# One-core attention and gated-MLP kernel: chunk 1's transposes moved from TensorE to DMA, the gate weights queued later, score runs joined, and a new instruction order

## The chip, the cores and the metric

The kernel runs on one core of a Trainium2 chip. The metric is device time in microseconds (us). The engines are named as the profile names them: PE (TensorE matmuls; PEld its weight loads), DVE (VectorE), ACT (ScalarE), POOL (GpSimd) and SP (SyncE, which here only issues DMAs). POOL issues DMAs too.

## The reference

```python
def layernorm(x): return (x - mean(x)) / sqrt(var(x) + 1e-5)

# x is 1 x 2048 x 512, bf16
q, k, v = split(layernorm(x) @ wqkv)           # 32 heads of 16 channels
# each position s attends to 8 positions: s, s-2, s-4, ..., s-14 (those below 0 masked)
logits = einsum("bhsd,bhswd->bhsw", q, k_gathered) * 16 ** -0.5
o = einsum("bhsw,bhswd->bhsd", softmax(logits), v_gathered)
h = x + o @ wo
gate, up = layernorm(h) @ W_gate, layernorm(h) @ W_up    # 512 -> 1376
out = h + (relu(gate) * up) @ W_down                     # 1376 -> 512
```

## The kernel before

The 2048 positions are worked in four chunks (`tk` 0 to 3) of 512, each of four blocks of 128 rows (`j` 0 to 3). In each chunk:

- `layernorm` makes the normed rows (tiles `row`; steps `xst`, `xag`, `xrl`, `xre`, `xn`). They are then transposed, channels onto partitions, into a `quad` tile `[128, 4, 512]`. Which way a pair of blocks is turned is listed in `DMAT`: a listed pair is turned by DMA transposes that SP issues (`f_td`, L533), any other on PE (`f_tp`, L544), whose PSUM bank is then copied out by ACT or, for block 1 of chunk 0, by DVE (`f_ev`, L558 and L560). Before, `DMAT` has chunk 3's second layernorm input of the attention (`('x',3,0)`, `('x',3,2)`) and all four second layernorms (`'h'`), not chunk 1's.
- The q, k and v projections (L585) run on PE, four matmuls of 512 columns to a bank, and ACT copies each bank out (L593). For chunk 0 the first six q and k banks are filled in parts as the blocks arrive: part `a` is block 0, `d` block 1, both with the first two weight tiles; `b` the other two weight tiles for blocks 0 and 1; `c` and `e` blocks 2 and 3.
- DVE multiplies q with shifted k (L636, L651 in chunk 0), for two halves (`hf` 0 and 1) of four shifts each. PE sums the products over channels with the 0/1 matrix `sel`: four matmuls of 32 output rows side by side in the array (`tile_position`). These are the **score runs** (`f_sc`, L642; L694 where DVE has added two products first, `PRE`). Each half had a run of its own. ACT takes the exponential (L708) into an `ex` tile.
- PE sums the exponentials (L725), ACT inverts the sum (L731, L734), `ex` is spread over partitions by DMAs (L768, from SP and POOL), and DVE multiplies with shifted v (L800, L815). The eight products are summed by DMAs that accumulate, issued by POOL (L843), and by DVE (L803), into the output tile `OT` (L807, L837).
- PE applies `wo` (L881), DVE adds x (L892), the second layernorm follows (ACT L457, DVE L510, DMA transposes), and then the MLP: up and gate matmuls (L954; the last 96 channels L921), ACT copies (L958, L961), DVE product (L982), down matmuls (L1005) and the output.

All weights are loaded by SP's queue. Before, `wo` (L348) and the gate half of `wgu_sb` (L349) go out in `setup`; the names in `LATE` (`u`, `d`) are loaded when chunk 0's attention is through.

What sets the order of the instructions: every step is an `Op` with an engine and a planned duration. `Plan.order` takes the steps by the numbers in `RANK`, gives each a planned start (from planned durations such as `SW`, the cost of a score run beyond its matmuls, and planned arrival times `XT` and `WT` of the blocks of x and the weights), and the program is written out by planned start. Each engine then works through its own list in that order and waits on semaphores; nothing overtakes on an engine or on SP's queue.

Of the kernel before, what the change touches and what calls it, by code (L numbers as in the profile page):

```python
# [8 lines left out]
P = 128  # L9
# [4 lines left out]
ALU = mybir.AluOpType  # L14
# [187 lines left out]
def kernel(  # L202
# [27 lines left out]
    LATE = "ud"  # L230
# [75 lines left out]
    def f_load(n, i):  # L306
        if n == "d":
            lo, hi = (0, 5) if i == 0 else (5, NFF)
            nc.sync.dma_start(
                wd_sb[:, lo:hi, :], B_W_down[lo * P:hi * P, :].rearrange("(ft p) n -> p ft n", p=P))  # L310
            if FTAIL and i:
                nc.sync.dma_start(wd_sb[:FTAIL, NFF, :], B_W_down[NFF * P:F, :])
        else:
            w = B_W_up.rearrange("(dt p) f -> p dt f", p=P)
            nc.sync.dma_start(wgu_sb[:, 2 * i:2 * i + 2, 1, :], w[:, 2 * i:2 * i + 2, :])

    def setup():
# [31 lines left out]
        nc.sync.dma_start(wgu_sb[:, :, 0, :], B_W_gate.rearrange("(dt p) f -> p dt f", p=P))  # L349

# [29 lines left out]
    XT = (3.45, 3.65, 4.05, 5.3, 7.15, 8.65, 9.0, 9.4, 13.0, 14.5)  # L380
    WT = (8.35, 8.35, 7.0, 10.85, 15.8, 25.5, 19.2, 29.0)
    DMAT = (('h',0,0),('h',0,2),('h',2,0),('h',2,2),('h',3,0),('h',3,2),('h',1,0),('h',1,2),('x',3,0),('x',3,2))
# [8 lines left out]

    BCN = 4
# [4 lines left out]
    TMT = (0, 1, 2, 3)  # L397
    TTM, DTG, ATE = 0.0825, 0.27, 0.225
# [6 lines left out]
    SW = 0.21  # L405
# [24 lines left out]
    fills = [add(("warm", 0), "PE", 5.6, f_warm, [], -500, take=[wb])]  # L430

# [8 lines left out]
    def layernorm(tk, src, dst_slots, pr, groups, on_act, residual=None):  # L440
# [7 lines left out]
        for grp in groups:  # L448
# [78 lines left out]
            for j0 in range(lo, hi, step):  # L527
# [24 lines left out]
                tev = not residual and tk == 0 and j0 == 1  # L552
# [15 lines left out]
    for tk in range(NCK):  # L568
# [52 lines left out]
        kp = {t: kdone.get((tk - 1, t)) for t in range(NT)}  # L621
        for hf in range(2):
# [55 lines left out]
            elif (tk, hf) in PRE:  # L678
# [19 lines left out]
                scd = [add(("sc%d" % hf, tk), "PE", nu * MM + SW, f_sc, [a], apr, take=[sc], use=[prd[0][1]], lat=PEL)]  # L698
# [8 lines left out]
            def f_ex(sc=sc, ex=ex):  # L707
                nc.scalar.activation(out=ex.t[:], in_=sc.t[:], func=ACT.Exp, scale=SCALE)  # L708

            def f_mk(hf=hf, ex=ex):  # L710
                V.tensor_tensor(out=ex.t[:, 0:PADL], in0=ex.t[:, 0:PADL], in1=mask[:, hf, :],
                                op=ALU.mult)

            a = add(("ex%d" % hf, tk), "ACT", A5, f_ex, scd, apr, take=[ex], use=[sc], lat=AL)
            if tk == 0:
                a = add(("mk%d" % hf, tk), "DVE", DSM, f_mk, [a], apr, use=[ex], lat=DL)
# [378 lines left out]
```

## Time and profile before

| | before |
|---|---|
| three runs | 191.16, 191.26, 192.79 us; median 191.26 us |
| span of the profiled execution | 190.2 us, granted clock 0.998 |
| between span and median | 1.06 us |
| busy: PE, DVE, ACT, POOL | 185.1, 150.7, 113.5, 25.2 us |
| PE matmuls | 1127 |

A row of the timeline reads: start and duration in us, engine, line, operation, output<-input, shape, count, and in brackets the idle time just before and what ended it. The duration of a group runs to the end of its last instruction; successive matmuls overlap, so what a matmul costs is the distance from one start to the next. The span is that of the one profiled execution; no time outside the profile is given for it, so it stands beside the median of the three runs with 1.06 us around it.

### The profile page before, as it was taken

Reading aid. Unit: us, or ns where it says so; the run is one execution under the profiler, and the core shown is the slowest. Engines: PE = TensorE matmul, PEld = TensorE weight load, DVE = VectorE, ACT = ScalarE, POOL = GpSimd, SP = SyncE. Lnnn points to the kernel's source line nnn. Section 1 sums busy time; section 2 is a strip of 40 time slices with the busy share of each in tenths; the row PEclk is TensorE's granted clock in tenths of the full one; section 3 lists DMA queues with packets and bytes.
Section 4 is the critical chain, followed back from the end, with each engine's and each line's share of the span. In section 5 each row is a group of like instructions: output and inputs, shape, how many; then the busy total and the mean of one; then the engine's idle time right before and its main releaser. Section 6 shows DMA issues by size and latency. Waiting matters only on the chain.

```text
span 190.2 us, 3080 instructions
## 1 busy us (share of the span) xinstructions
PE 185.1 (97%) x1127; PEld 95.4 (50%) x1127; DVE 150.7 (79%) x231; ACT 113.5 (60%) x234; POOL 25.2 (13%) x47
## 2 busy tenths in 40 slices
PE   7799999999999999999999999999999999999993
PEld 7676555554444445544344464444454444455453
DVE  5899999999999999999999998998485712114324
ACT  2579999985467945762483795146466713358500
POOL 4000221400000004230033123027000000000000
PEclk9999999999999999999999999999999999999999
DMA  5999364993198858998438798779922211000503
GB/s 182 281 347 370 90 163 87 191 194 59 21 330 177 233 166 153 194 191 182 83 65 152 142 181 186 180 137 166 221 44 55 55 28 59 28 0 0 165 3 110
DMA packets 27743, 26.98 MB, mean 142 GB/s; under 512 B 14704, under 2 KB 23248, under 8 KB 27728
## 3 DMA queue, kind: packets, MB, share of 16 engines
q1 hardware_dynamic: 23696, 15.34, 29.7%
q0 software_dynamic: 3312, 10.49, 28.6%
q10 hardware_dynamic: 720, 0.95, 1.5%
q8 instruction: 9, 0.15, 0.3%
q14 instruction: 6, 0.05, 0.1%
HBM read 8.42 MB, written 2.10 MB: 55 GB/s over the span
## 4 chain that ended last, share of the span: by engine, by line
PE 82%; ACT 11%; DMA 3%; DVE 1%; issue 1%; SPq 0%
PE bank L954 37%; PE bank L1005 20%; PE bank L585 12%; PE bank L881 7%; ACT row L512 5%; DMA x_sm<-in_A_x_dram 3%; PE bank L921 3%; ACT quad L560 2%; ACT vT L593 2%; PE bank L642 2%; ACT quad L593 1%; PE bank L694 1%; ACT kT L593 1%; ACT ex L708 1%; SPq L323 0%
## 5 line engine op out<-in xcount | busy, mean ns | idle before, releaser
L954 PE MATMUL bank<-quad,wgu_sb 128*128 128x512 bf16 x320 | 72.3, 379 | 0.0
L954 PEld LDWEIGHTS <-wgu_sb 128*128 128x128 bf16 x320 | 30.9, 98 | 37.3 <-issue 1.7
L1005 PE MATMUL bank<-wd_sb,gT 128*128 128x512 bf16 (+3 forms) x198 | 39.7, 355 | 0.0
L958 ACT CAST up_sb<-bank 128x512 bf16<-128x512 f32 x40 | 23.1, 591 | 21.0 <-PE bank L954 14.9
L585 PE MATMUL bank<-quad,wqk_sb 128*128 128x512 bf16 (+2 forms) x176 | 30.4, 321 | 0.5 <-DVE quad L558 0.4
L961 ACT ACTIVATE gr<-bank 128x512 bf16<-128x512 f32 x40 | 23.3, 606 | 9.7 <-PE bank L954 8.2
L1005 PEld LDWEIGHTS <-gT 128*128 128x128 bf16 (+1 forms) x198 | 18.5, 98 | 19.7
L982 DVE TENSOR_TENSOR gT<-gr,up_sb 128x1024 bf16<-128x1024 bf16 x20 | 13.6, 686 | 14.4 <-PE bank L1005 7.0
L636 DVE TENSOR_TENSOR big<-quad,kT 128x4096 bf16<-128x4096 bf16 x11 | 24.8, 2279 | 0.0
L585 PEld LDWEIGHTS <-wqk_sb 128*128 128x128 bf16 x176 | 17.1, 113 | 11.4 <-issue 1.1
L800 DVE TENSOR_TENSOR big<-big,vT 128x4096 bf16<-128x4096 bf16 x9 | 20.4, 2281 | 0.0
L843 POOL DMA_DIRECT2D big<-big x13 | 11.6, 965 | 64.3 <-PE bank L954 32.6
L1013 DVE SCALAR_TENSOR_TENSOR row<-bank,iv,x_sm 128x512 bf16<-128x512 f32 (+2 forms) x10 | 6.3, 643 | 13.4 <-PE bank L1005 13.2
L457 ACT ACTIVATE junk<-x_sm,sm 128x512 bf16<-128x512 bf16 x16 | 11.6, 727 | 8.8 <-DVE x_sm L892 8.8
L585 PE MATMUL bank<-quad,wv_sb 128*128 128x512 bf16 x64 | 16.1, 380 | 0.2 <-ACT quad L560 0.2
L881 PE MATMUL bank<-wo_sb,quad 128*128 128x512 bf16 x64 | 15.0, 379 | 0.0
L892 DVE SCALAR_TENSOR_TENSOR x_sm<-x_sm,bank 128x512 bf16<-128x512 bf16 x16 | 10.8, 678 | 2.4 <-PE bank L881 2.4
L803 DVE TENSOR_TENSOR big<-big 128x1024 bf16<-128x1024 bf16 (+1 forms) x17 | 10.3, 622 | 1.6 <-DMA big<-big 1.4
L467 DVE BATCH_NORM_STATS2 st<-x_sm 128x6 f32<-128x512 bf16 x16 | 10.2, 679 | 1.1 <-DMA x_sm<-in_A_x_dram 1.1
L593 ACT CAST quad<-bank 128x512 bf16<-128x512 f32 x16 | 9.3, 594 | 2.5 <-PE bank L585 2.4
L593 ACT CAST kT<-bank 128x512 bf16<-128x512 f32 x16 | 9.3, 596 | 1.9 <-PE bank L585 1.0
L593 ACT CAST vT<-bank 128x512 bf16<-128x512 f32 x16 | 9.1, 610 | 2.1 <-PE bank L585 2.1
(80 smaller groups left out, 175.6 us busy)
## 6 DMA issues: line engine op xcount, KB each, us to landing
big<-big POOLq DMA_DIRECT2D x13, 512.0 KB, 5.2
big<-ex SPq DMA_DIRECT2D x20, 128.0 KB, 3.1
big<-ex POOLq DMA_DIRECT2D x12, 128.0 KB, 3.8
wgu_sb<-in_B_W_gate_dram SPq DMA_DIRECT2D x1, 1376.0 KB, 9.3
wgu_sb<-in_B_W_up_dram SPq DMA_DIRECT2D x2, 688.0 KB, 5.0
wd_sb<-in_B_W_down_dram SPq DMA_DIRECT2D x2, 640.0 KB, 5.7
x_sm<-in_A_x_dram SPq DMA_DIRECT2D x2, 512.0 KB, 6.2
wqk_sb<-wqk_sb POOLq DMA_DIRECT2D x2, 512.0 KB, 5.8
```

The source lines that it names most:

```text
L457: nc.scalar.activation(out=junk[:, j % 2, :], in_=h.t[:] if h else x_sm[:, tk * BPC + j, :], func=ACT.Square, bias=sm.t[:, j:j + 1], scale ...
L585: nc.tensor.matmul(mm.t[:, lo:hi], lhsT=wv_sb[:, dt, t:D:NT] if c == 2 else wqk_sb[:, dt, c * D + t:(c + 1) * D:NT], rhs=xnT.t[:, dt, lo:h ...
L593: nc.scalar.copy(out=o, in_=mm.t[:])
L636: V.tensor_tensor(out=pb.t[:].rearrange("p (t w) s -> p t w s", t=2), in0=q4, in1=k4, op=ALU.mult)
L800: V.tensor_tensor(out=mt.t[:], in0=ab.t[:], in1=v8, op=ALU.mult)
L843: nc.gpsimd.dma_start(mt.t[:, 0:4, :], mt.t[:, 4:8, :], accum_op=ALU.add)
L881: nc.tensor.matmul(od.t[:], lhsT=OT.t[:, t, j * P:(j + 1) * P], rhs=wo_sb[:, t, :], start=(t == 0), stop=(t == NT - 1 and tk not in RPE))
L954: nc.tensor.matmul(mm.t[:fs, lo:hi], lhsT=wgu_sb[:, dt, g, ft * P: ft * P + fs], rhs=hnT.t[:, dt, lo:hi], start=(dt == 0), stop=(dt == NT ...
L958: nc.scalar.copy(out=ub.t[:fs, i, :], in_=um.t[:fs, :])
L961: nc.scalar.activation(out=gr.t[:fs, i, :], in_=gm.t[:fs, :], func=ACT.Relu)
L982: V.tensor_tensor(out=gt.t[:fs, 0:n, :], in0=gr.t[:fs, 0:n, :], in1=ub.t[:fs, 0:n, :], op=ALU.mult)
L1005: nc.tensor.matmul(od.t[:, c0:c1], lhsT=gts[ft].t[:fs, ft % 2, j * P:(j + 1) * P], rhs=wd_sb[:fs, ft, c0:c1], start=(ft == 0), stop=(ft == ...
```

## The change

Five edits: chunk 1's first layernorm goes into `DMAT` (transposes by SP's DMAs in place of PE and ACT); the gate weights join `LATE` as `g` and their load is planned as a step of SP after `wo`; in the chunks listed in `MS` (1 to 3) both halves' score matmuls become one step, `sc1`; `TEV = ()` lets ACT copy out block 1 of chunk 0 where DVE did; `RANK`, `SW`, `XT` and `WT` have new numbers.

```diff
 RANK = [
-    0, 1, 2, 3, 4, 5, 6, 7, 8, 9, 18, 10, 11, 12, 14, 15, 16, 17, 13, 19,
+    0, 4, 5, 7, 22, 38, 56, 20, 33, 120, 41, 15, 25, 97, 135, 406, 441, 493, 11, 224,
...
-    LATE = "ud"
+    LATE = "udg"
...
+        elif n == "g":
+            nc.sync.dma_start(wgu_sb[:, :, 0, :], B_W_gate.rearrange("(dt p) f -> p dt f", p=P))
...
         nc.sync.dma_start(wo_sb[:], A_wo.rearrange("(p t) f -> p t f", t=NT))
-        nc.sync.dma_start(wgu_sb[:, :, 0, :], B_W_gate.rearrange("(dt p) f -> p dt f", p=P))
-
+        if "g" not in LATE:
+            f_load("g", 0)
...
-    XT = (3.45, 3.65, 4.05, 5.3, 7.15, 8.65, 9.0, 9.4, 13.0, 14.5)
-    WT = (8.35, 8.35, 7.0, 10.85, 15.8, 25.5, 19.2, 29.0)
-    DMAT = (('h',0,0),('h',0,2),('h',2,0),('h',2,2),('h',3,0),('h',3,2),('h',1,0),('h',1,2),('x',3,0),('x',3,2))
+    XT = (3.5, 3.7, 4.6, 6.3, 7.3, 8.3, 8.6, 8.95, 13.1, 14.5)
+    WT = (7.95, 7.95, 6.2, 11.2, 15.8, 25.5, 19.2, 29.0)
+    DMAT = (('h',0,0),('h',0,2),('h',2,0),('h',2,2),('h',3,0),('h',3,2),('h',1,0),('h',1,2),('x',1,0),('x',1,2),('x',3,0),('x',3,2))
...
+    MS = (1, 2, 3)
...
+    TEV = ()
...
-    SW = 0.21
+    SW = 0.19
...
+    if "g" in LATE:
+        wload["g"].append(add(("ldg", 0), "SP", 0.45, lambda: f_load("g", 0), wload["o"], 0, lat=1.0, dq=(1.0, 3.6)))
...
-                tev = not residual and tk == 0 and j0 == 1
+                tev = not residual and tk == 0 and j0 in TEV
...
+        both = []
         for hf in range(2):
...
+            elif tk in MS:
+                both.append((sc, ex, [a for a, _, _ in prd], [b for _, b, _ in prd], 4, lambda p=prd: [f() for _, _, f in p]))
             elif tk in MERGE:
...
+            if tk in MS and hf == 0:
+                continue
+            if tk in MS:
+                a = add(("sc1", tk), "PE", sum(x[4] for x in both) * MM + SW, lambda p=both: [x[5]() for x in p],
+                        [d for x in both for d in x[2]], apr, take=[x[0] for x in both], use=[d for x in both for d in x[3]], lat=PEL)
```

Three places show what the new order does.

**DVE at the start**, chunk 0's first layernorm: `st` and `mv` are statistics of a block of x, `row` its normed rows (`row_104` to `row_107` are blocks 0 to 3; `quad_79<-bank_140` copies block 1's transpose out). Before:

```order
L515 TENSOR_SCALAR row_104<-x_sm,mv_117,rs_129 128x512
L467 BN_STATS st_115<-x_sm 128x6
L515 TENSOR_SCALAR row_105<-x_sm,mv_117,rs_129 128x512
L470 BN_AGGR mv_117<-st_115 128x2
L467 BN_STATS st_116<-x_sm 128x6
L470 BN_AGGR mv_117<-st_116 128x2
L558 COPY quad_79<-bank_140 128x4x128
L515 TENSOR_SCALAR row_106<-x_sm,mv_117,rs_129 128x512
L515 TENSOR_SCALAR row_107<-x_sm,mv_117,rs_129 128x512
```

and of the change:

```order
L478 BN_AGGR mv_117<-st_115 128x2
L478 BN_AGGR mv_117<-st_114 128x2
L523 TENSOR_SCALAR row_104<-x_sm,mv_117,rs_129 128x512
L475 BN_STATS st_116<-x_sm 128x6
L478 BN_AGGR mv_117<-st_116 128x2
L523 TENSOR_SCALAR row_105<-x_sm,mv_117,rs_129 128x512
L523 TENSOR_SCALAR row_106<-x_sm,mv_117,rs_129 128x512
L523 TENSOR_SCALAR row_107<-x_sm,mv_117,rs_129 128x512
```

Block 2's statistics (`st_115`) now precede block 0's rows, block 1's rows stand behind the statistics of block 3 (`st_116`), and the copy is gone from DVE.

**SP's queue** between the loads of `setup` and the second layernorm: `big_92<-ex` are the spreading DMAs of chunk 0, `quad_82<-row` chunk 2's transposes. Before:

```order
L768 DMA big_92<-ex_101 128x1x512 x2
L533 DMA_TRANSPOSE quad_82<-row_107 128x4x128
L533 DMA_TRANSPOSE quad_82<-row_108 128x4x128
L533 DMA_TRANSPOSE quad_82<-row_104 128x4x128
L533 DMA_TRANSPOSE quad_82<-row_105 128x4x128
L315 DMA wgu_sb<-in_B_W_up_dram 128x2x1376 x2
```

and of the change (`quad_81` is chunk 1):

```order
L541 DMA_TRANSPOSE quad_81<-row_106 128x4x128
L541 DMA_TRANSPOSE quad_81<-row_105 128x4x128
L791 DMA big_92<-ex_100 128x1x512 x2
L791 DMA big_92<-ex_101 128x1x512 x2
L541 DMA_TRANSPOSE quad_82<-row_107 128x4x128
L541 DMA_TRANSPOSE quad_82<-row_108 128x4x128
L541 DMA_TRANSPOSE quad_82<-row_105 128x4x128
L541 DMA_TRANSPOSE quad_82<-row_106 128x4x128
L314 DMA wgu_sb<-in_B_W_gate_dram 128x4x1376
L317 DMA wgu_sb<-in_B_W_up_dram 128x2x1376 x2
```

Chunk 1's transposes (the last two are shown) now precede the spreading DMAs, and the gate load has moved behind chunk 2's transposes.

**PE at chunk 1's scores**: `bank_143<-big_92` ends the run of the first half, `wv_sb` is a projection. Before:

```order
L642 MATMUL bank_143<-big_92,sel 32x512
L642 LDWEIGHTS sel
L642 MATMUL bank_143<-big_92,sel 32x512
L585 LDWEIGHTS wv_sb
L585 MATMUL bank_139<-quad_84,wv_sb 128x512
```

and of the change, where `bank_139` is the first half and `bank_142` the second:

```order
L651 LDWEIGHTS sel
L651 MATMUL bank_139<-big_89,sel 32x512
L651 LDWEIGHTS sel
L651 MATMUL bank_142<-big_90,sel 32x512
L651 LDWEIGHTS sel
```

The second half's matmuls now follow the first's at once, where a projection stood between.

More of the change, by code (lines that the diff above doesn't have):

```diff
@@ L696, in f_sc @@
                                              stop=(u == nu - 1), tile_position=(0, g * HB))
-                scd = [add(("sc%d" % hf, tk), "PE", nu * MM + SW, f_sc, [a], apr, take=[sc], use=[prd[0][1]], lat=PEL)]
+                if tk in MS:
+                    both.append((sc, ex, [a], [prd[0][1]], nu, f_sc))
+                else:
+                    scd = [add(("sc%d" % hf, tk), "PE", nu * MM + SW, f_sc, [a], apr, take=[sc], use=[prd[0][1]], lat=PEL)]
+            elif tk in MS:
+                both.append((sc, ex, [a for a, _, _ in prd], [b for _, b, _ in prd], 4, lambda p=prd: [f() for _, _, f in p]))
             elif tk in MERGE:
@@ L705, with f_ex, f_mk @@
                                    take=[sc], use=[pb], lat=PEL))
[L707 to L716, printed above, removed]
-            exs.append(ex)
-            exd.append(a)
+            if tk in MS and hf == 0:
+                continue
+            if tk in MS:
+                a = add(("sc1", tk), "PE", sum(x[4] for x in both) * MM + SW, lambda p=both: [x[5]() for x in p],
+                        [d for x in both for d in x[2]], apr, take=[x[0] for x in both], use=[d for x in both for d in x[3]], lat=PEL)
+                scs = [(h, x[0], x[1], [a]) for h, x in enumerate(both)]
+            else:
+                scs = [(hf, sc, ex, scd)]
+            for h, sc, ex, scd in scs:
+                def f_ex(sc=sc, ex=ex):
+                    nc.scalar.activation(out=ex.t[:], in_=sc.t[:], func=ACT.Exp, scale=SCALE)
+                def f_mk(h=h, ex=ex):
+                    V.tensor_tensor(out=ex.t[:, 0:PADL], in0=ex.t[:, 0:PADL], in1=mask[:, h, :],
+                                    op=ALU.mult)
+                a = add(("ex%d" % h, tk), "ACT", A5, f_ex, scd, apr, take=[ex], use=[sc], lat=AL)
+                if tk == 0:
+                    a = add(("mk%d" % h, tk), "DVE", DSM, f_mk, [a], apr, use=[ex], lat=DL)
+                exs.append(ex)
+                exd.append(a)
         dn, rc = Buf(at_s), Buf(rc_s)
@@ L863 @@
             lg = add(("lg", tk), "DVE", 0.08, f_lg, list(oev.values()), apr, use=[OT], lat=0.1)
-            for n in LATE:
+            for n in LATE.replace("g", ""):
                 for i in range(2):
```

74 rows, old and new, of the table RANK are left out of this document.

## The prediction

> **What bounds the kernel now.** I read the busy table first, then the waits of PE after the start, then the table by stages, and then went to the places that the change touches.
>
> ```profile
> PE 185.1 (97%) x1127; PEld 95.4 (50%) x1127; DVE 150.7 (79%) x231; ACT 113.5 (60%) x234; POOL 25.2 (13%) x47
> PE bank L585 <- ACT quad L560: 0.2, 1, 0.2
> 10.48:37.70 27.22, 27.05 (x200) 16.07 (x200) 27.02 (x45) 25.57 (x47) 5.21 (x8) 1.00 0.74 206
> 37.70:90.00 52.30, 52.30 (x292) 24.94 (x292) 52.05 (x69) 33.58 (x70) 6.34 (x9) 1.00 0.77 173
> 143.00:187.70 44.70, 44.29 (x237) 21.86 (x235) 16.25 (x33) 19.83 (x44) 0.00 (x0) 1.00 0.18 49
> ```
>
> The second row is the whole list of PE's waits from 16 us to the end: one. In the stage rows (length, then busy us of PE, PEld, DVE, ACT, POOL, then granted clock) PE is full in every stage at clock 1.00, so the kernel ends when PE's list is through, and a saving is what leaves that list or closes a gap in it. But DVE is as full until 90 us (27.02 of 27.22, 52.05 of 52.30): PE runs without gaps because its order always has a matmul ready where DVE is late. The two meet at chunk 0's `wo`:
>
> ```profile
> 47.53 0.76 DVE L807 TENSOR_TENSOR quad<-big,rec 128x512 bf16<-128x512 bf16 x2
> 48.29 3.62 PE L881 MATMUL bank<-wo_sb,quad 128*128 128x512 bf16 x16
> ```
>
> DVE writes the last of chunk 0's attention output at 47.53 + 0.76 = 48.29, and `wo` starts at 48.29. A PE that gets there sooner has to wait.
>
> **The change part by part.** The sum is made against the profiled execution's span, 190.2 us; 1.06 us lie between it and the median of 191.26, and I take them as unchanged.
>
> *Transposes leave PE.*
>
> ```profile
> 32.73 0.61 PE L544 MATMUL bank<-identity,row 128*128 128x128 bf16 x8
> 34.95 0.61 PE L544 MATMUL bank<-identity,row 128*128 128x128 bf16 x8
> 35.40 1.92 PE L585 MATMUL bank<-quad,wqk_sb 128*128 128x512 bf16 x8
> ```
>
> Eight cost the distance to the next start, 35.40 - 34.95 = 0.45, or 0.056 each. Chunk 1 has 16 of them: **-0.90**. That is certain, since PE's list is shorter by it.
>
> *Score runs joined.* A run of 16 matmuls in chunk 1, and chunk 2's two runs (timeline rows; the fourth row is a piece of the chain of waits):
>
> ```profile
> 43.74 1.03 PE L585 MATMUL bank<-quad,wqk_sb 128*128 128x512 bf16 x4
> 44.69 1.05 PE L642 MATMUL bank<-big,sel 128*32 128x512 bf16 x16
> 45.67 1.05 PE L585 MATMUL bank<-quad,wv_sb 128*128 128x512 bf16 x4
> 59.27 8.63 PE bank L954 x40
> 67.83 1.05 PE L642 MATMUL bank<-big,sel 128*32 128x512 bf16 x16
> 68.70 0.60 PE L694 MATMUL bank<-big,sel 128*32 128x512 bf16 x8
> ```
>
> A 512-column matmul costs 8.63 / 40 = 0.216. The four at 43.74 are through at 44.60, the run starts at 44.69 (0.09), and its 16, four side by side, are 4 x 0.216 = 0.86 of the 0.98 to the next start (0.12): 0.21 a run beyond its matmuls. But in chunk 2 the second run starts 68.70 - 67.83 = 0.87 after the first: these two are joined already, and nothing goes there. Chunks 1 and 3 save one run each: 2 x 0.21 = **-0.41**, where the edit reads like three.
>
> *ACT's queue in chunk 1.*
>
> ```profile
> 19.83 1.00 ACT L560 COPY quad<-bank 128x1024 bf16<-128x1024 bf16 x1
> 21.20 1.03 ACT L560 COPY quad<-bank 128x1024 bf16<-128x1024 bf16 x1
> 37.16 0.38 PE L725 MATMUL bank<-row,spread 128*128 128x512 bf16 x1
> 37.70 0.59 PE L585 MATMUL bank<-quad,wv_sb 128*128 128x512 bf16 x2 [0.16 <-ACT quad L560]
> ```
>
> Two copies of 1.0 us leave an engine that is 25.57 us busy in 27.22. The one gap that ACT makes on PE, 37.70 - 37.16 - 0.216 = 0.32, should close: **-0.32**, bounds -0.32 and 0.
>
> *The start.* Here the order costs. These rows are before's (timeline; the last but one is from the chain of waits):
>
> ```profile
> 6.23 0.40 DVE L515 TENSOR_SCALAR row<-x_sm,mv,rs 128x512 bf16<-128x512 bf16 x1
> 6.69 0.40 PE L544 MATMUL bank<-identity,row 128*128 128x128 bf16 x4 [0.52 <-DVE row L515]
> 7.33 0.69 DVE L467 BATCH_NORM_STATS2 st<-x_sm 128x6 f32<-128x512 bf16 x1 [0.61 <-DMA x_sm<-in_A_x_dram]
> 7.37 0.83 PE L585 MATMUL bank<-quad,wqk_sb 128*128 128x128 bf16 x12
> 8.15 0.39 DVE L558 COPY quad<-bank 128x512 bf16<-128x512 bf16 x1
> 8.46 0.79 DVE L515 TENSOR_SCALAR row<-x_sm,mv,rs 128x512 bf16<-128x512 bf16 x2
> 9.36 1.07 ACT L560 COPY quad<-bank 128x512 bf16<-128x512 bf16 x2 [0.56 <-PE bank L544]
> 10.48 5.54 PE bank L585 x54
> 15.84 1.89 PE L585 MATMUL bank<-quad,wv_sb 128*128 128x512 bf16 x8
> ```
>
> Block 3 of x lands at 7.3, and its statistics start then in both orders. Before, block 1's rows were made at 6.23, ahead of that wait, and PE filled it at 7.37 with part `a` of six banks. Now block 1's rows stand behind it: they take the copy's place at 8.15 (so moving the copy to ACT by itself costs and saves nothing on DVE), block 2's follow at 8.46 and block 3's at 8.85, as before. Block 1's transpose starts at about 8.59 and not 6.69. ACT then has three copies in a row from 9.03 at 0.49 each (1.07 for two less the overlap), the last to 10.59, and PE, which has the transposes and three parts `a` still to do, reaches the matmuls that need it at about 10.68 rather than 10.48. Behind that point stand 5.36 us in the old order (15.84 - 10.48), and 0.33 more now, the six 0.056 us matmuls of part `a` that no longer fit ahead of it. Chunk 0's q and k end at 10.68 + 5.36 + 0.33 = 16.37 rather than 15.84: **+0.53**. Bounds: 0, if block 3 lands early enough to cover it, and +0.9, if a copy more slips.
>
> *Chunk 1 by DMA.* Four transposes run beside nothing at 120 us and beside the up weights at 52 us:
>
> ```profile
> L533 SPq DMA_TRANSPOSE quad<-row x4: 1212/1220/1222, 120.8 to 124.7; - x4
> DMA to landing us min/median/max: 2.5/2.5/2.5
> DMA to landing us min/median/max: 2.6/3.9/5.2
> 16.52 2.93 ACT L512 ACTIVATE row<-x_sm,nb,rs 128x512 bf16<-128x512 bf16 x4
> 22.35 0.62 PE L585 MATMUL bank<-quad,wv_sb 128*128 128x512 bf16 x2
> ```
>
> SP issues one every 1.3 us ((124.7 - 120.8) / 3), and one lands after 2.5. ACT makes chunk 1's rows at 0.73 each; the last two now stand behind chunk 0's last q copy, which follows the q and k end by 0.7 (to 17.1), so the last row is there at 18.7. SP issues the third transpose at 18.7 and the fourth at 20.0, which lands at 22.5; the gate load no longer runs then, so I take the 2.5. PE gets to chunk 1's first projection (22.35 before) at 22.35 + 0.53 - 0.90 = 22.0: it waits **+0.5**. Bounds 0 and +1.9 (landing after 3.9). The spreading DMAs of chunk 0 queue behind on SP: the fourth transpose is issued by 21.4, where DVE's mask on `ex` now also is, so they lose nothing.
>
> Other moves: the gate load now follows chunk 2's transposes at about 31.7, and PE needs it after 59; as a transfer it is hidden (see the rival). Putting both halves into `sc1` holds four product buffers until one run; chunk 1's first exponential comes some 6 us later, but the sum over both halves waited for the second before, so nothing waits longer. I price both at 0.
>
> **Sum:** -0.90 - 0.41 - 0.32 + 0.53 + 0.50 = -0.60. The meeting point allows it: PE reaches `wo` at about 48.29 - 0.21 - 0.32 + 0.53 + 0.50 = 48.8 (the transposes that went are replaced ahead of it by projections), while DVE, whose first product starts 0.2 later, is there at 48.5. The rest of the gain lies behind that point. Time: 191.26 - 0.60 = **190.7**.
>
> **The rivals.**
>
> *The start costs nothing and PE gains it all.* If block 3 lands early and the transposes are in time, the sum is -1.63. But DVE is at chunk 0's output at 48.3 at the soonest, where PE would be at 47.8: 0.5 is given back in a wait there. That gives -1.1, 190.1 us; without that wait 189.6.
>
> *Slower than before: the gate load meets the accumulating DMAs.*
>
> ```profile
> L843 POOL DMA_DIRECT2D big<-big x4: 852/898/1190, 32.2 to 37.2; - x4
> DMA to landing us min/median/max: 4.6/5.9/8.1
> wgu_sb<-in_B_W_gate_dram SPq DMA_DIRECT2D x1, 1376.0 KB, 9.3
> 46.86 0.76 DVE L803 TENSOR_TENSOR big<-big 128x512 bf16<-128x512 bf16 x2
> ```
>
> Chunk 0's four accumulating transfers of 512 KB go out at 32 to 37, the last lands at 37.2 + 8.1 = 45.3, and DVE uses it from 46.3 (the step before the row at 46.86). From 1 us of delay on, DVE, then `wo`, then PE are late. The gate load (1376 KB, 9.3 us beside x) now starts at 31.7, in the midst. The transposes beside the up loads went from 2.5 to a median of 3.9 and a worst of 5.2, so a delay of 1.4 to 2.7 is in the trace; at 2.7 `wo` would start at 48.5 + 1.7 = 50.2, 1.4 later than in my sum: 192.1 us. Against it: an accumulating transfer is itself the larger part of the traffic, and the load can wait. [...]
>
> *PE's clock falls back.* PE would do next to nothing between 7.1 and 8.6 and only some 1.1 us of matmuls between 5.7 and 9.1. A run at half clock for 3.4 us costs 1.7 us, so 190.7 + 1.7 = 192.4. The stage rows show 1.00 throughout, with gaps of up to 0.7 before 8.6, so the trace has no such fall. [...]
>
> **How the numbers follow.** The sum (with 0.4 to either side for new small waits): 0.55. The full gain: 0.17. The gate load: 0.20. The clock: 0.05. The rest, 0.03, is further off. The range takes the low end 189.6 from the first rival and 192.1 from the second. A difference within 1%, 189.35 to 193.17, is about what a measurement tells from no change; most of my cases lie inside: faster 0.08, same 0.88, slower 0.04.
>
> **What would show it.** PE's matmul count falls by 16. Chunk 0's first v projection starts near 16.4 (15.84); at 15.8 or less the start is mispriced. A wait of PE on DMA transposes stands near 22. No wait on ACT near 37. One gap of 0.2 is gone in chunk 1 and in chunk 3, and none in chunk 2. `wo` of chunk 0 starts at 48.8; past 49.5, with DVE waiting on `big<-big`, the gate load is to blame. What would make it wrong most easily is a new wait of DVE in chunks 1 to 3, which would push a later `wo` and so PE.

## The result: 207.0 us, 7.2% slower, and the profile after

The changed kernel takes 207.0 us (median of four executions), against 191.4 for the kernel before on the same chip: 1.072 times as long (95% interval 1.065 to 1.079), where 190.7 us were predicted. The ratios here and below are taken to the kernel before, run beside on the same chip, and leave disturbed executions out (two took 1100 us), which the medians do not, so "by its ratio" means the ratio times the time of the kernel before beside it. The profiled execution has a span of 203.2 us (before 190.2); it is the shortest of the four (205.0 us), and what follows accounts for its 13.0 us of span.

First the busy row of the page of after, then all its waits of PE, then the stages (length, busy us of PE, PEld, DVE, ACT and POOL, granted clock, DMA share, GB/s):

```profile
PE 186.0 (92%) x1093; PEld 95.1 (47%) x1111; DVE 150.9 (74%) x230; ACT 112.5 (55%) x233; POOL 25.2 (12%) x47
```

```profile
PE bank L977 <- DMA quad<-row: 3.7, 1, 3.7
PE bank L904 <- DVE quad L830: 1.8, 1, 1.8
PE bank L593 <- DMA quad<-row: 1.3, 1, 1.3
PE bank L904 <- DVE quad L860: 1.0, 1, 1.0
PE bank L433 <- DVE warm L329: 1.0, 1, 1.0
PE bank L977 <- ACT junk L465: 0.9, 1, 0.9
PE bank L703 <- DVE big L689: 0.9, 1, 0.9
PE bank L748 <- DVE row L763: 0.7, 1, 0.7
PE bank L651 <- DVE big L660: 0.7, 1, 0.7
PE bank L552 <- DVE row L523: 0.6, 2, 0.4
```

```profile
10.48:37.70 27.22, 24.78 (x170) 14.04 (x172) 26.42 (x44) 22.69 (x44) 4.45 (x7) 1.00 0.72 168
37.70:90.00 52.30, 48.50 (x269) 23.16 (x272) 47.77 (x57) 32.48 (x67) 4.85 (x6) 1.00 0.73 175
90.00:143.00 53.00, 47.03 (x236) 22.00 (x239) 44.81 (x59) 25.82 (x56) 11.38 (x16) 0.97 0.68 140
143.00:187.70 44.70, 44.49 (x210) 20.53 (x212) 19.26 (x35) 22.73 (x48) 2.58 (x3) 1.00 0.30 65
```

PE does the same work (186.0 us busy, before 185.1) but is no longer full: it lacks 2.4, 3.8 and 6.0 us in the first three stages, and 0.2 in the fourth. The list of its waits had one entry after 16 us and now has eight, nearly all on DVE or on a DMA. PEld has 16 loads less (1127 to 1111), which is the 16 transposes; of its 1111 matmuls 1093 are recorded.

Counted from start to start over all matmuls after 15 us, ten gaps of more than 0.3 us beyond a matmul's own time sum to 13.8 us (before: two, 0.65). PE's list after 15 us is 1.4 us shorter (0.9 of transposes; chunk 0's q and k are also 0.4 further on by then, since x landed earlier in this execution), small gaps are 0.2 less, and 1.4 us go in a stretch at half clock (0.50 from 139.07 to 142.48): 13.2 - 1.4 - 0.2 + 1.4 = 13.0, the difference of the spans.

| from | place | gap | late |
|---|---|---|---|
| 18.1, 18.6, 21.5 | chunk 0's score runs | 2.0 | DVE's products (L660) |
| 22.3 | chunk 1's first projection | 1.6 | DMA transposes |
| 50.3 | chunk 0's `wo` | 1.9 | DVE, behind the accumulating DMAs |
| 59.9, 88.1 | chunk 1's sum of exponentials, its `wo` | 2.1 | DVE |
| 99.1, 110.0 | chunk 1's MLP; second half of chunk 3's joined scores | 2.3 | ACT; DVE (L689) |
| 135.5 | chunk 2's MLP | 3.9, then half clock | DMA transposes |

**Chunk 0's `wo`.** The accumulating DMAs of chunk 0 (the view of their line in after; its second row is who waited for them: us, times), and `wo` in the timelines of DVE and PE:

```profile
L866 POOL DMA_DIRECT2D big<-big x4: 852/898/1185, 32.0 to 38.0; - x4
  DVE big L826: 3.7, 2
DMA to landing us min/median/max: 6.5/9.4/11.9
```

```profile
51.95 0.75 DVE L830 TENSOR_TENSOR quad<-big,rec 128x512 bf16<-128x512 bf16 x2
50.06 0.59 PE L904 MATMUL bank<-wo_sb,quad 128*128 128x512 bf16 x2
52.43 3.31 PE L904 MATMUL bank<-wo_sb,quad 128*128 128x512 bf16 x14 [1.77 <-DVE quad L830]
```

The transfers that landed 4.6 / 5.9 / 8.1 us after issue now take 6.5 / 9.4 / 11.9. DVE waits 3.7 us for them in two waits and, where it was to be through at 48.5, is through at 52.7. `wo` starts at 50.1, and its third matmul has to wait for DVE.

**Chunk 2's second layernorm.** The line of its four transposes, POOL's timeline, PE's timeline, and two stretches of the stage view:

```profile
L541 SPq DMA_TRANSPOSE quad<-row x4: 1211/1218/1255, 129.5 to 134.1; - x4
DMA to landing us min/median/max: 2.4/2.5/5.3
```

```profile
133.79 0.91 POOL L866 DMA_DIRECT2D wqk_sb<-wqk_sb  x1 [7.78 <-DVE wqk_sb L823]
```

```profile
139.52 1.86 PE L977 MATMUL bank<-quad,wgu_sb 128*128 128x512 bf16 x4 [3.74 <-DMA quad<-row]
```

```profile
135.60:139.40 3.80, 0.18 (x3) 0.04 (x1) 2.60 (x3) 0.17 (x1) 0.77 (x1) 0.95 1.08 193
139.40:142.40 3.00, 2.88 (x12) 1.71 (x12) 0.39 (x1) 0.00 (x0) 0.00 (x0) 0.50 0.49 126
```

Three of the transposes land 2.4 to 2.5 us after issue; the last goes out at 134.1, just behind an accumulating DMA of 133.8, and takes 5.3. PE waits 3.74 us and then runs at half clock (0.50) until 142.5. In the kernel before these transposes stood at 120.8 to 124.7, all at 2.5, and PE did not wait for them.

### The profile page after: what moved, and what is told of

Same layout as the page of the kernel before. It is cut to its first block, busy times and chain, and to the rows that moved or that the text cites. A ratio compares the mean times of both kernels' runs of the same rounds, so it can differ in the third digit from the quotient of the medians.

```text
span 203.2 us, 3039 instructions
## 1 busy us (share of the span) xinstructions
PE 186.0 (92%) x1093; PEld 95.1 (47%) x1111; DVE 150.9 (74%) x230; ACT 112.5 (55%) x233; POOL 25.2 (12%) x47
## 4 chain that ended last, share of the span: by engine, by line
PE 33%; DVE 30%; DMA 18%; issue 13%; POOL 2%; SPq 1%; ACTq 0%; DVEq 0%; POOLq 0%
PE bank L977 19%; PE bank L1028 9%; DMA big<-big 7%; DVE big L645 7%; DVE big L660 4%; DMA big<-ex 3%; DVE big L823 3%; DVE x_sm L915 3%; DMA quad<-row 3%; DMA wqk_sb<-in_A_wqkv_dram 2%; DVE wqk_sb L823 2%; DMA x_sm<-in_A_x_dram 2%; DVE big L838 2%; DVE big L826 2%; PE bank L904 2%
## 5 line engine op out<-in xcount | busy, mean ns | idle before, releaser
L1028 PE MATMUL bank<-wd_sb,gT 128*128 128x512 bf16 (+4 forms) x195 | 39.8, 355 | 0.2
L593 PE MATMUL bank<-quad,wqk_sb 128*128 128x512 bf16 (+2 forms) x172 | 29.0, 320 | 0.2
L645 DVE TENSOR_TENSOR big<-quad,kT 128x4096 bf16<-128x4096 bf16 x12 | 27.2, 2280 | 0.0
L465 ACT ACTIVATE junk<-x_sm,sm 128x512 bf16<-128x512 bf16 x16 | 11.5, 721 | 17.7 <-DVE x_sm L915 17.6
L826 DVE TENSOR_TENSOR big<-big 128x1024 bf16<-128x1024 bf16 (+2 forms) x19 | 12.2, 660 | 8.8 <-DMA big<-big 8.7
L593 PE MATMUL bank<-quad,wv_sb 128*128 128x512 bf16 x61 | 15.3, 380 | 1.4 <-DMA quad<-row 1.3
L823 DVE TENSOR_TENSOR big<-big,vT 128x4096 bf16<-128x4096 bf16 x6 | 13.5, 2285 | 0.0
L904 PEld LDWEIGHTS <-quad 128*128 128x128 bf16 x64 | 6.0, 98 | 11.4 <-DVE quad L830 2.5
L823 DVE TENSOR_TENSOR big<-wqk_sb,vT 128x4096 bf16<-128x4096 bf16 x4 | 9.1, 2287 | 2.8 <-DMA wqk_sb<-ex 2.8
L593 PEld LDWEIGHTS <-wv_sb 128*128 128x128 bf16 x64 | 7.0, 114 | 9.0 <-issue 3.6
```

What stands on the lines that cost most here:

```text
L465: nc.scalar.activation(out=junk[:, j % 2, :], in_=h.t[:] if h else x_sm[:, tk * BPC + j, :], func=ACT.Square, bias=sm.t[:, j:j + 1], scale ...
L593: nc.tensor.matmul(mm.t[:, lo:hi], lhsT=wv_sb[:, dt, t:D:NT] if c == 2 else wqk_sb[:, dt, c * D + t:(c + 1) * D:NT], rhs=xnT.t[:, dt, lo:h ...
L645: V.tensor_tensor(out=pb.t[:].rearrange("p (t w) s -> p t w s", t=2), in0=q4, in1=k4, op=ALU.mult)
L823: V.tensor_tensor(out=mt.t[:], in0=ab.t[:], in1=v8, op=ALU.mult)
L826: V.tensor_tensor(out=mt.t[:, 0:n, :], in0=mt.t[:, 0:n, :], in1=mt.t[:, n:2 * n, :], op=ALU.add)
L904: nc.tensor.matmul(od.t[:], lhsT=OT.t[:, t, j * P:(j + 1) * P], rhs=wo_sb[:, t, :], start=(t == 0), stop=(t == NT - 1 and tk not in RPE))
```

## The experiments

Names beginning with `b` are the kernel before with one or more of the edits, those with `a` the changed kernel with edits undone. `RANK` keeps the relative order of its parent; a step that only one of them has gets the place named.

### The gate load

`b_gate_late`, SP's queue of the kernel before:

```diff
 DMA wo_sb<-in_A_wo_dram
-DMA wgu_sb<-in_B_W_gate_dram 128x4x1376
 ... spreading DMAs of chunk 0, four DMA transposes
+DMA wgu_sb<-in_B_W_gate_dram 128x4x1376
```

Three theories were set up together, for this run, `a_gate_early` and `b_edits`: in theory 1 the gate load is the whole loss; in theory 2 the new order or the joined scores are, and the load only happens to lie there; in theory 3 there are two losses, the load at chunk 0's `wo` and the order behind it.

> The kernel before, with only the gate load moved: from setup to behind the four DMA transposes that go out between 27 and 31 us. Order and all else as before. Theory 1: accumulating transfers of chunk 0 take 6.5 to 12 us instead of 4.6 to 8, wo starts near 53 to 54, and since nothing behind it has slack the time is 203 to 207. Theory 2: 191 to 192. Theory 3: 196 to 198.

196.5 us, ratio 1.024 (1.019 to 1.028). The load alone costs 4.5 us: theory 3's range, not that of 1 or 2. Its accumulating DMAs (view of their line):

```profile
L866 POOL DMA_DIRECT2D big<-big x4: 852/899/1187, 31.6 to 36.6; - x4
  DVE big L826: 4.2, 2
DMA to landing us min/median/max: 9.3/10.6/12.4
```

The median landing went from 5.9 to 10.6, and DVE waits 4.2 us for them.

`b_gate_half`: half of the bytes there, the other half in `setup`.

```diff
 setup:
-            f_load("g", 0)
+        nc.sync.dma_start(wgu_sb[:, 0:2, 0, :], B_W_gate...[:, 0:2, :])
 f_load, behind the four transposes:
-            nc.sync.dma_start(wgu_sb[:, :, 0, :], B_W_gate...)
+            nc.sync.dma_start(wgu_sb[:, 2:4, 0, :], B_W_gate...[:, 2:4, :])
```

> The kernel before; the gate load is cut in two: the first half (688 KB) in setup, the second half (688 KB) behind the four DMA transposes near 31 us. With the whole load there, chunk 0's four accumulating transfers landed 3.7 to 4.3 us later than in the kernel before and the time rose by 2.35% (4.5 us). Theory S (the 16 DMA engines are shared, so every byte put beside the transfers delays them by its own transfer time): about half, landings 1.8 to 2.2 us later, of which 0.8 to 1 is slack: the time 1 to 2 us above before, 193.4 to 194.5. Theory O (it is the order, one load ahead of the transfers delays them by a fixed amount whatever its size): 4 us later again, 196 to 197. If small loads are free: 192 to 192.5.

193.8 us, ratio 1.010 (1.006 to 1.015).

```profile
L865 POOL DMA_DIRECT2D big<-big x4: 852/899/1187, 32.4 to 37.4; - x4
DMA to landing us min/median/max: 6.6/7.6/9.9
```

The median landing is 1.7 later with half of the load and 4.7 with all, the time 2.0 and 4.5 us (from the ratios): here the cost grew with the bytes (688 and 1376 KB). In time it is about half for half, as theory S had it, in landings a little less than its 1.8 to 2.2; the fixed cost of theory O is out.

`a_gate_early`, and the same again for its trace as `a_gate_early2`:

```diff
         nc.sync.dma_start(wo_sb[:], A_wo.rearrange("(p t) f -> p t f", t=NT))
-        if "g" not in LATE:
-            f_load("g", 0)
+        nc.sync.dma_start(wgu_sb[:, :, 0, :], B_W_gate.rearrange("(dt p) f -> p dt f", p=P))
```

> The changed kernel with the gate load put back behind the load of wo in setup; every other instruction stands where the change has it. Theory 1 (the gate load among chunk 0's accumulating transfers is the whole loss): the accumulating transfers land 4.6 to 8 us after issue as before, wo of chunk 0 starts near 49, and the time is the prediction's 190.7 (189.6 to 192.1). Theory 2 (the new order or the joined scores are to blame, the load only happens to lie there): 204 to 207, with wo of chunk 0 near 54. Theory 3 (two losses: the gate load for the 6 us at chunk 0's wo, the order for the 7 us that come behind it): wo near 49, but the time 197 to 200.

> The changed kernel with the gate load in setup once more, for a trace of it. 203 to 204 as timed. If the order or the joined scores cost the rest, the four accumulating transfers of chunk 0 land 4.6 to 8 us after issue, yet wo of chunk 1 stands at 88 or later, and it is a DVE wait between 50 and 85 that shows why; if the spreading DMAs of chunk 0 behind the transposes cost it, chunk 0's wo is already at 50 or later.

203.8 us, ratio 1.059 (1.055 to 1.062), and 202.4 in the one execution of `a_gate_early2`, whose trace is used here. Theory 1 is out, and theory 3 too hopeful (it had 197 to 200; the time is next to theory 2's 204 to 207, the place of `wo` is theory 3's): undoing the load takes back 1.3 of 7.2 points, a fifth. The trace has what was expected of the transfers:

```profile
L865 POOL DMA_DIRECT2D big<-big x4: 854/898/1192, 31.4 to 37.4; - x4
DMA to landing us min/median/max: 4.6/4.9/6.9
```

`wo` of chunk 0 starts at 49.2 and that of chunk 1 at 85.4 (before 48.3 and 85.5), close to the prediction, and not at 88 or later as was expected for chunk 1. Chunk 2's starts at 121.3 (117.7) and chunk 3's at 153.6 (142.5): what is lost here is lost behind 85 us.

### The edits in the old order

`b_ms` (joined scores alone), `b_dmat` (chunk 1 by DMA alone), `b_edits` (both, and `TEV = ()`), `b_dmat_gl` (`b_dmat` with the gate load late). All begin from the kernel before:

```diff
 b_ms, b_edits
+    MS = (1, 2, 3)
 b_dmat, b_edits, b_dmat_gl
-    DMAT = (('h',0,0), ... ('h',1,2),('x',3,0),('x',3,2))
+    DMAT = (('h',0,0), ... ('h',1,2),('x',1,0),('x',1,2),('x',3,0),('x',3,2))
 b_dmat_gl
-    LATE = "ud"
+    LATE = "udg"
```

> The kernel before, in its order, with one edit: both halves' score matmuls of chunks 1 to 3 in one step, so that the first half's matmuls and its exponential wait until all four products are made. Theory A (joined scores are free, as priced): 191 to 192. Theory B (they hold four product buffers and both PSUM banks until the last product, so that the products and trees behind them on DVE, and then the exponentials on ACT, come late in each of three chunks): 194 to 199, with a new wait of DVE or of POOL for a product buffer at chunk 1.

> The kernel before, in its order, with one edit: chunk 1's first layernorm turned by four DMA transposes, each issued by SP as soon as its normed rows are there, and all ahead of the spreading DMAs of chunk 0, as in the changed kernel. Theory A (PE gains 0.9 and waits about 0.5 near 22): 190.5 to 192. Theory C (SP's queue: four transposes of 1.3 us each stand ahead of the spreading DMAs, these start 2 to 4 us later, DVE's first product with v and the accumulating transfers with them, and chunk 0's wo moves by as much): 194 to 197, with DVE waiting for the spreading DMAs near 25 to 28 and wo of chunk 0 at 51 to 53.

> The order before (its RANK, SW, XT and WT), the gate load in setup as before, but with chunk 1's first layernorm turned by DMA, both halves' scores in one step in chunks 1 to 3 and block 1's copy on ACT. Theory 1: 190 to 192, for what the edits take off PE (0.9 and 0.4) minus small waits. Theory 2, if the edits and not the order are to blame: over 197; if the order: 190 to 192. Theory 3: 190 to 192.

> The kernel before, in its order, with two edits: chunk 1 turned by DMA (alone: +2.6%, PE waits 3.7 us for transposes that run beside the gate load and take 4 to 5 us) and the gate load late (alone: +2.35%). If the two losses only add: 201 to 202. Theory T (the transposes are late because the gate load runs beside them): with the load out of their way they land 2.5 us after issue, PE's wait falls under 2 us, no stretch at half clock follows, and most of the first loss goes: 197 to 198.5.

`b_ms`: 192.8 us, ratio 1.003 (1.001 to 1.006). The joined scores are free to 0.3%, theory A; but they bring nothing either.

`b_dmat`: 197.0 us, ratio 1.026 (1.020 to 1.032). Slower as theory C had it, but not by its mechanism: no wait of DVE on the spreading DMAs is in its list. PE itself waits for the transposes (PE's waits, the transposes' line, and two stretches of the stage view):

```profile
PE bank L593 <- DMA quad<-row: 3.7, 1, 3.7
```

```profile
L541 SPq DMA_TRANSPOSE quad<-row x4: 1217/1476/1667, 17.1 to 21.6; - x4
DMA to landing us min/median/max: 3.8/4.1/5.0
```

```profile
21.80:25.40 3.60, 0.01 (x3) 0.00 (x0) 3.25 (x10) 1.07 (x2) 1.28 (x3) 1.00 0.97 163
25.80:29.20 3.40, 3.40 (x10) 1.23 (x9) 1.02 (x3) 1.35 (x4) 0.00 (x0) 0.50 0.68 186
```

3.7 of wait, 3.4 / 2 = 1.7 for the half clock, less 0.9 of transposes: 4.5, of 5.1 measured.

`b_edits`: 201.6 us, ratio 1.048 (1.041 to 1.054), where 190 to 192 or over 197 was expected. In it the fourth transpose stands behind two spreading DMAs on SP's queue, and PE waits 5.8 us for the transposes. In the change it stands ahead of them, so this time does not measure what the edits cost in the change's order.

`b_dmat_gl`: 201.8 us, ratio 1.051 (1.047 to 1.054). The two losses add (1.026 and 1.024), and theory T is wrong: with the load out of the way PE still waits 3.6 us.

```profile
L541 SPq DMA_TRANSPOSE quad<-row x4: 1225/1416/2128, 17.6 to 22.5; - x4
DMA to landing us min/median/max: 3.2/3.7/4.2
```

The transposes are issued too late for PE (17.6 to 22.5) and land later than the 2.5 us at 120.8 to 124.7 in before: median 4.1 with the load in `setup`, 3.7 with it late.

### The later part

`a_store`, `a_es2`, `a_pe_x1` are `a_gate_early` with one place mended each, `a_mend` has all three:

```diff
 a_store, SP's queue at chunk 2's second layernorm
 DMA_TRANSPOSE quad<-row
-DMA out_dram<-x_sm 128x2x512
 DMA_TRANSPOSE quad<-row (three)
+DMA out_dram<-x_sm 128x2x512
 a_es2, DVE at chunk 2
+row<-ex,ex  (sum of exponentials; ex<-ex,rec and the spreading DMAs behind it)
 big<-quad,kT  (chunk 3's first product)
 ... chunk 1's sums, its residual adds
-row<-ex,ex
 a_pe_x1
-    DMAT = (... ('x',1,0),('x',1,2), ...)
+    DMAT = (...)
```

> The changed kernel with the gate load in setup (203.8 when timed, ratio 1.059), and one DMA moved on SP's queue: the store of chunk 0's blocks 0 and 1 goes behind chunk 2's four second-layernorm transposes instead of between the first and the second. Theory Q (the last transpose is issued at 130.3, 0.5 after an accumulating transfer went out, takes 5.3 us instead of 2.5, and PE waits 3.8 us and then runs 3.4 us at half clock): the three later transposes go out 0.6 to 0.7 earlier, the last one before the accumulating transfer, and lands near 132; PE's wait falls from 3.8 to about 0.5 and the slow stretch goes: 4 to 5 us faster, 198 to 200. Theory D (DVE sets the pace of chunks 2 and 3, the transposes only hide it): PE waits elsewhere, 1 us gained at most, 202 to 203.

> As the changed kernel with the gate load in setup, with chunk 2's sum of exponentials, its inverse, the product with it and the spreading DMAs moved ahead by about 8 us (sum before chunk 3's first product, spreading DMAs at 83 to 84 us instead of 94), about where the kernel before has them. Theory D: DVE's wait of 2.9 us on the spreading DMAs (before its first product with v in chunk 2) is gone, all that follows in chunks 2 and 3 comes 2 to 3 us earlier: 200.5 to 202. Theory Q: the wait goes, but chunk 2's transposes still meet the accumulating transfer, so that PE's long wait and slow stretch stay, and 0 to 1.5 us are gained: 202 to 204.

> As the changed kernel with the gate load in setup, with chunk 1's first layernorm turned on PE again (two pairs, among chunk 0's v projections) instead of by DMA; all else in the new order. PE gets 16 transposes of 0.056 us more (0.9). Theory T (the DMA transposes are late beside the gate load, PE waits 1.4 us for them, and the spreading DMAs behind them are late too): 201.5 to 203, that is 1 to 2 faster than with the DMA transposes. If they cost nothing in this order: 204 to 205.

> All three mends together, in the new order with the gate load in setup and the scores joined: chunk 1 turned on PE, chunk 2's spreading DMAs earlier, the store behind chunk 2's transposes. If these three places are what the new order costs, they add up to 7 to 9 us: 194 to 197, within 1 to 2.5% of the kernel before. If not, something spread over chunks 1 to 3 is left: 199 or more.

`a_store`: 200.5 us, ratio 1.033 (1.024 to 1.042), 2.6 points better; by its ratio 198.2 us, as theory Q had it, but the four executions lie from 197.3 to 205.8. Its profiled execution, 5 us longer than the median, shows the last transpose at 134.6 still behind an accumulating DMA (2.4/2.5/5.3) and PE still waiting 3.4 us. The time speaks for Q, that trace does not, so I count it as half a proof.

`a_es2`: 203.4 us, ratio 1.050 (1.041 to 1.059). In its trace the spreading DMAs go out at 88 to 90 us, not at the 83 to 84 aimed at; DVE's wait on them is gone from its list, and PE's wait for the transposes is still there (3.4 the longest), as theory Q had it. The time decides nothing: the gain of 0.9 points is inside the two intervals, the median lies in theory Q's range and the 201.6 us by its ratio in theory D's.

`a_pe_x1`: 202.9 us, ratio 1.048 (1.036 to 1.060): 1.1 points better. The median lies in theory T's range (201.1 us by its ratio, just below it), but the two intervals overlap, so this run alone does not show a gain; `a_old_tail_pe` below does.

`a_mend`: 197.4 us, ratio 1.026 (1.018 to 1.035), 3.2 points better; 194 to 197 was expected, or 199 and more. In its profiled execution, 3 us longer than the median, chunk 2's transposes are clean (their line), and another pile-up appears behind them (waits of DVE, and DMA issues from 127 to 150):

```profile
L540 SPq DMA_TRANSPOSE quad<-row x4: 1217/1220/1227, 123.8 to 127.7; - x4
DMA to landing us min/median/max: 2.4/2.6/2.7
```

```profile
DVE big L825 <- DMA big<-big: 8.9, 3, 7.5
```

```profile
big<-big POOLq DMA_DIRECT2D x3, 512.0 KB, 12.1
gT<-row SPq DMA_TRANSPOSE x1, 11.7
```

Three accumulating DMAs (median 12.1 us) and a transpose (11.7) meet there. The three mends together fall short of a full repair: 2.6 points are left. That the rest is lost in such meetings of DMAs is likely from this trace, but not shown.

The whole of the later part is tested from the other side. `a_old_tail` has every edit of the change and its order up to the step that the kernel before does at 67 us (chunk 2's scores); from there on the steps stand in the order of before. `a_old_tail_ge` has the gate load in `setup` besides, `a_old_tail_pe` also chunk 1 on PE:

```diff
 a_old_tail, a_old_tail_ge, a_old_tail_pe
     RANK: steps that stand before chunk 2's scores in the order before: as in the change
-          the other steps: as in the change
+          the other steps: as before
```

> The changed kernel with all its edits, the gate load late; its new order is kept for what the kernel before does until chunk 2's scores (67 us), and from there on the steps stand in the order of the kernel before. Theory L (two losses: the gate load and the transposes until chunk 0's wo, and the new order of chunks 2 and 3 for the rest): wo of chunk 0 ends near 55 as in the changed kernel, and that loss of about 4 us is all that is left: 195.5 to 198. If the later losses are only the early ones carried on: 203 to 207, as the changed kernel.

> The same with the gate load in setup. Theory L: chunk 0's wo ends at 52 to 53 (0.9 later than in the kernel before), chunk 2's spreading DMAs and chunk 2's transposes stand as in the kernel before, no wait of PE over 2 us after 60: 192 to 194, that is all but 1 us of the loss of 11 us undone by the order of the later part. If the early part or the edits cost the rest: 199 or more.

> The kernel with the change's early order and the later part in the order of before, the gate load in setup (with DMA transposes 1.018 of the kernel before, PE waiting 1.9 to 2.3 us for them and then 3.4 us at half clock), and chunk 1 turned on PE again. If the DMA transposes are what is left of the loss: 1.8% goes and 0.9 us of PE time comes back, 191.5 to 193.5, the same as the kernel before within 1%. If the early order or the joined scores cost it: 195 or more.

| kernel | us | ratio (95%) |
|---|---|---|
| the change | 207.0 | 1.072 (1.065 to 1.079) |
| `a_old_tail` | 199.9 | 1.033 (1.027 to 1.040) |
| `a_old_tail_ge` | 195.8 | 1.018 (1.012 to 1.023) |
| `a_old_tail_pe` | 193.6 | 1.009 (1.006 to 1.013) |

`a_old_tail` came out just above theory L's range (198.4 us by its ratio) and well below the carried-on loss: chunk 0's `wo` ends at 57.4 rather than 55, since PE waits 3.2 us for DVE there and then runs at half clock (0.50 from 53.58 to 56.99). `a_old_tail_ge` is above its range too (195.4 by its ratio). In its profiled execution, 2 us longer than the median, PE waits up to 1.9 us for chunk 1's transposes, with half clock behind it (its rows are in the last section), so that trace shows more of this loss than a usual execution has. `a_old_tail_pe` is within 1% of the kernel before, near the upper end of what was expected if the DMA transposes are the rest. Step by step, of 7.2 points: **3.9 are the order of the later part, 1.6 the gate load, 0.8 the DMA transposes of chunk 1** (from unrounded ratios, each uncertain by 0.6 to 0.9 points); 0.9 are left for the early order and the joined scores: 0.3 by `b_ms`, about 0.3 for the start (0.55 us, next section), and a rest below the uncertainty, whose cause stays open. Taken in the other sequence (the gate load undone first) the load comes to 1.3 and the later part to 4.1; alone in the old order the load costs 2.4, so the shares hold for this sequence of steps. No version beat the kernel before.

## Why the prediction was wrong, point by point

- *PE bounds, and a saving is what leaves its list.* True of the kernel before; but the change left PE with too little in front of the places where DVE and DMAs are late. The 0.9 us of transposes did leave the list, and the -0.90 called certain still came out as a loss: with them back on PE, `a_old_tail_pe` is 0.8 points faster. Without them chunk 0's score runs lose 2.0 us to DVE's products in after and 0.9 in `a_old_tail_ge`; in `a_old_tail_pe`, the same with the transposes back, no gap above 0.3 us is left there: the transposes had filled that time.
- *The start, +0.53.* Right, though the sign named for it did not show: chunk 0's first v projection starts at 15.4 in after, not near 16.4 (15.8 before). Block 3 of x landed earlier there: its statistics start at 6.37, and at 7.33 before. From that start to the first v projection it is 8.51 to 8.52 us in before and in the five runs `b_ms`, `b_dmat`, `b_dmat_gl`, `b_gate_late` and `b_gate_half`, and 9.06 to 9.08 in eight traces of the new order: 0.55 more at the same arrival. Added to before's 7.33, 9.07 gives the 16.4 of the prediction. The start of block 3's statistics differs from execution to execution (6.1 to 8.1 in the traces), by more than the term. DVE and PE in after:

```profile
6.37 0.69 DVE L475 BATCH_NORM_STATS2 st<-x_sm 128x6 f32<-128x512 bf16 x1
15.44 2.75 PE L593 MATMUL bank<-quad,wv_sb 128*128 128x512 bf16 x11
```

- *Score runs, -0.41.* In the old order they bring nothing (1.003). In the change the joined run of chunk 3 starts with its first half and waits 0.9 us for the second, which stood 12 us later before.
- *ACT's gap near 37, -0.32.* Right: no wait of PE on `ACT quad` is left.
- *Chunk 1 by DMA, +0.5.* The wait is 1.3, inside the bounds of 0 to 1.9. The step took 2.5 us a landing; the later pair took 4.2 and 3.4.
- **The gate load, priced at 0.** The first step that failed. The rival had the mechanism, the place and the sign ("past 49.5, with DVE waiting on `big<-big`, the gate load is to blame" is what the trace shows), but took 1.4 to 2.7 us of delay from transposes beside the up loads. The median delay is 3.5 in after and 4.7 alone. An estimate of the most that it could cost stood in the rows: the load took 9.3 us beside x.
- **Everything behind chunk 1 priced at 0.** The larger failure, 3.9 of 7.2 points. The prediction looked at three places of the new order, and named "a new wait of DVE in chunks 1 to 3" as what might go wrong, but gave it no price and left the slower side 0.04. The order shows it: chunk 2's sum of exponentials stands behind two of chunk 1's residual adds, and its spreading DMAs go out at 97.7 instead of 80.4 (their line in before, then in after), so that DVE waits for them (its waits in after):

```profile
L768 POOL DMA_DIRECT2D big<-ex x4: 567/589/602, 80.4 to 82.1; - x4
```

```profile
L791 POOL DMA_DIRECT2D wqk_sb<-ex x4: 567/588/598, 97.7 to 99.3; - x4
```

```profile
DVE big L823 <- DMA wqk_sb<-ex: 2.8, 1, 2.8
```

- *PE's clock, 0.05 at the start.* In after it fell, but at 139 us and behind another wait; it stayed at 0.50 for 3.41 us, the 3.4 that this rival took. Between 5.70 and 9.10 after had 2.75 us of matmuls, not 1.1, and the clock was 1.00 until 20. In the profiled execution of `a_pe_x1`, where block 3 of x landed late, it fell where this rival had it: 1.03 us of matmuls between 5.97 and 9.38, then half clock, and the first v projection at 18.7, 10.6 after block 3's statistics and not 9.1. DVE's row for block 3 there, and two stretches of the stage view:

```profile
8.12 0.69 DVE L474 BATCH_NORM_STATS2 st<-x_sm 128x6 f32<-128x512 bf16 x1 [1.68 <-DMA x_sm<-in_A_x_dram]
```

```profile
5.97:9.38 3.41, 1.03 (x15) 0.67 (x12) 1.69 (x7) 1.66 (x6) 0.00 (x0) 1.00 0.84 272
9.38:12.79 3.41, 3.40 (x29) 3.16 (x30) 3.34 (x9) 1.86 (x4) 0.00 (x0) 0.50 0.96 302
```

- *The 1.06 us between span and median.* Most executions listed with both show 1.7 to 1.8 us between their time and their span (the change: 204.97 and 203.2). It is the same on both sides, and no number hangs on it.
- The four transposes at 27 to 31 us that the text ahead calls chunk 2's are those of chunk 3's first layernorm (`('x',3,0)`, `('x',3,2)`); chunk 2's first layernorm is turned on PE at 32.7. No number hangs on it.

## What to carry to other kernels

When a schedule is replaced, price the order itself: for every engine that is near full, list what each late consumer waits for in the new order, not only at the places of the edits. A transfer that is "hidden" for its own consumer can still cost those that transfer beside it, here 2.0 us for 688 KB and 4.5 for 1376, so ask what is in flight when it starts and who has no slack. An engine that is full without gaps may depend on the fillers between its waits: here PE's waits at chunk 0's score runs (2.0 us in after) appeared when the transposes left.

## What the runs showed of the hardware

**Half clock after a stretch that was not idle.** In after the clock was 0.50 from 139.07 to 142.48, 3.41 us; in `a_gate_early2` it was 0.50 for twice that, from 134.05 to 140.87. Two neighbouring stretches of `a_old_tail_ge`, then of `a_es2`, cut where the granted clock changes or, in the second, at the same spacing:

```profile
21.32:24.73 3.41, 1.41 (x19) 0.45 (x12) 3.41 (x12) 1.88 (x4) 1.30 (x2) 1.00 0.94 86
24.73:28.14 3.41, 3.19 (x9) 1.23 (x9) 2.34 (x6) 1.70 (x5) 1.08 (x2) 0.50 0.85 253
```

```profile
137.23:140.64 3.41, 1.48 (x12) 1.00 (x12) 1.29 (x2) 0.00 (x0) 0.00 (x0) 1.00 0.99 209
140.64:144.05 3.41, 3.41 (x19) 1.61 (x17) 2.59 (x3) 2.31 (x5) 1.73 (x2) 1.00 0.19 38
```

With 1.41 us of matmuls in the first stretch (41%) the next ran at half clock, with 1.48 (43%) it did not. Other pairs, cut in the same way:

| kernel | stretch, us | matmuls in it, us | clock of the next 3.41 us |
|---|---|---|---|
| after | 135.65 to 139.07 | 0.13 | 0.50 |
| `a_es2` | 21.18 to 24.59 | 0.47 | 0.50 |
| `a_pe_x1` | 5.97 to 9.38 | 1.03 | 0.50 |
| `a_old_tail` | 50.17 to 53.58 | 1.13 | 0.50 |
| `a_gate_early2` | 130.64 to 134.05 | 1.21 | 0.50 |
| after | 50.30 to 53.71 | 1.64 | 1.00 |

The ends of matmuls are modelled, and some of their records are missing (18 of 1111 in after), so these shares are rough; what decides between the two outcomes is not shown. The four matmuls at 139.52 in after, at clock 0.50, took (141.18 - 139.52) / 4 = 0.415 us each from start to start, against 0.216 in before. By an estimate from these rows, 3.41 us at half clock cost a PE that is otherwise full 1.7 us (half of 3.41).

**A transpose issued with no other transfer under way that landed late.** In after the third of chunk 1's transposes was issued at 19.2, when no other transfer was under way, and landed 4.2 us later (2.5 in before at 120.8 to 124.7); most of its packets had moved by 21.2. Why the rest came late, and why `b_dmat_gl` has the same (3.2 to 4.2 us), stays open.
